# A two-layer transformer kernel on one core: twelve norm transposes go from TensorE to SyncE's DMA queue, and softmax pairs are allowed from an earlier point

## The chip, the cores and the metric

The kernel runs on one core of one Trainium2 chip. The metric is the device time of one execution in microseconds (us); a program's time is given as the median of its runs, and one execution of it is recorded by the hardware profiler. The engines are called PE (TensorE), DVE (VectorE), ACT (ScalarE), POOL (GpSimd) and SP (SyncE). SP only issues DMAs here.

## The reference, cut to what matters

```python
def attention(x):                      # A: wqkv, wo
    q, k, v = split(x @ wqkv)          # 32 heads of 16
    p = softmax(q @ k.T * 16 ** -0.5)
    return concat_heads(p @ v) @ wo

def dense(x):                          # B: w1, w2
    return relu(x @ w1) @ w2

x = A_x                                # [1, 2048, 512] bf16
for _ in range(2):
    x = x + attention(layernorm(x))
    x = x + dense(layernorm(x))
```

The inner width of `dense` is 1792. All inputs and the output are bf16. The softmax has 32 heads of 2048 x 2048 scores in each of the two layers: some 268 million exponentials in all, which is what most of the program's time goes to.

## The kernel before, in words

**Tiles.** The 2048 rows are cut into four chunks of 512 rows (`QS`), each of four row blocks of 128. In the second layer the last two chunks are cut in halves of 256 rows. Everything lives in SBUF: x as 16 tiles `x_t`, the transposed norm of a chunk as `xnT[j]` (128 x 4 x 512), keys as `ktp`, values as `vaug` (one tile of 128 rows for each key block, with columns of ones that give the softmax sums), and the attention output as `ot`.

**Norm.** Statistics of a row block come from DVE (`ln_stats`, L479), POOL works out the reciprocal root (`ln_seed`, L488 to L496), and DVE writes the normalised block into one of four buffers `xn0` to `xn3` (`ln_apply`, L526). In before, PE then transposes it, four 128 x 128 pieces a row block, into the PSUM bank `ps_f` (`ln_transpose`, L535), and DVE copies two row blocks at a time into `xnT[j]` (`ln_groups`, L583). As soon as PE has read an `xn` buffer, the next chunk's `ln_apply` may write it. The tag `("ln1", 0, j)` names the first norm of the first layer for chunk j; the code counts layers from 0. Chunk 0 of this norm is done by a short opening sequence of its own (L1146 to L1190), the other three go through `ln_rows` and, in before, `ln_groups`.

**Keys, values, queries.** `k_group`, `v_group` and `q_group` are groups of matmuls (L445) that read `xnT[j]`, write the one bank `ps_f`, and have it copied by DVE (L607 for keys, L643 for values, L657 for queries, which are masked and scaled on the way).

**Softmax by slots.** The main loop (from L1246) runs over slots. In each slot PE makes the scores of three blocks of 128 keys x 512 queries in one of two groups of three PSUM banks, `ps_s` (L1375), and ACT takes their exponentials with one instruction (L1384) into one of five buffers `e`. PE multiplies the result with the values (L963) into the bank `ps_o`. When a head is complete, DVE copies `ps_o` to `u` (L856, L875, L877), and a chain of small DMAs on SP's queue (`c<-u` at L882, `u<-c` at L905) and a broadcast DMA on POOL's queue (`r<-u` at L907) brings the reciprocal of the sums to all rows; DVE multiplies (L893).

**Pairs.** A slot may leave one of its three blocks to DVE. Then ACT's instruction covers 1024 columns instead of 1536. Two such blocks, from two slots two apart, form a pair: DVE computes an approximate exponential by steps named by their outputs: `lin` twice (L1070), `step` (L1111), `cube` (L1122), for some pairs a scaling (L1123), `step` again (L1111), and `cube` again (L1126). PE then adds three products to `ps_o` for each block of a pair, with `lin`, `step` and `cube`, in place of one with `e`. A condition in the main loop (L1273) decides whether a slot may begin a pair. In before, in the first layer, pairs are free only when the values of all 16 row blocks are made (`("v", 0, 15) in made`); until then a pair may begin only when no other is in work and the first keys of chunk 1 are there.

**Who sets the order.** Each engine runs its instructions in the order in which the program issues them. A planner in the kernel's Python code writes that order: it keeps its own clocks for PE and DVE (`now_pe`, `now_dve`), adds fixed costs for each task, and notes in `made` when each key will be there. `task` puts work into DVE's list, `mark` notes a key with a lag, `at` asks for the time of keys, `fill_pe` starts waiting groups on PE where their keys are made in time. These clocks only decide the order of the instructions; the chip's semaphores decide when they run.

**SP's queue at the start.** SP issues the loads of x (L176), of `wqkv`, `wo` and `w2` (L194, 1792 KB), and the first four blocks of `w1` (L695), in that order. The next DMA that SP issues in before is the first `c<-u`.

Of the kernel before, what the change touches and what calls it, by code (L numbers as in the profile page):

```python
# [25 lines left out]
def kernel(  # L26
# [10 lines left out]
    nc = tc.nc  # L37
    P = 128
# [13 lines left out]
    NQS = S // QS  # L52
    TPC = QS // P
# [17 lines left out]
    NP = 5  # L71
# [7 lines left out]
    FLOOR = 0.56  # L79
    C_LAG, R_LAG, U_LAG = 3600.0, 10500.0, 3000.0  # L80
    VLAG = 1
    RSTD_LAG = 4000.0
    AHEAD = (8.0, 8.0)
    LATE = 0.0
# [3 lines left out]
    PAIR_PACE = 2  # L88
# [47 lines left out]
    xnT = [sb([P, NDC, QS], BF16, f"xnT{j}") for j in range(NQS)]  # L136
# [104 lines left out]
    now_dve = [0.0]  # L241
# [3 lines left out]
    made = {}  # L245

    def mark(key, engine="dve", lag=0.0):
        made[key] = (engine, (now_pe if engine == "pe" else now_dve)[0] + lag)
# [38 lines left out]
    def task(cost, fn, makes=(), deps=(), place=None):  # L287
        t = {"cost": cost, "fn": fn, "makes": makes, "deps": deps}
        dve_q.insert(len(dve_q) if place is None else place, t)
        maker.update({k: t for k in makes})  # L290
# [178 lines left out]


    ln_seq = []

    def ln_n(tag):
        return ln_seq.index(tag) % 2
# [49 lines left out]
    def ln_apply(tag, tt, i):  # L524
        n = ln_n(tag)
        nc.vector.tensor_scalar(  # L526
            out=xnbuf[i][:], in0=x_t[tt][:],
            scalar1=mv[n][:, i, 0:1], scalar2=ya_[n][:, i : i + 1],
            op0=ALU.subtract, op1=ALU.mult,
        )  # L530

    def ln_transpose(tag, i, b=None, at_bank=None):
# [7 lines left out]
        mark(("xT", tag, i), "pe")  # L540
        return pt[:, 0 : NDC * P].rearrange("p (c f) -> p c f", c=NDC)

    def ln_rows(tag, tt, n, i):

        if tag not in ln_seq:
            ln_seq.append(tag)
        at_tag = ln_seq.index(tag)
        prev = ln_seq[at_tag - 1]
        rows_of_prev = chunks[prev[1:]][1]
        before_that = ln_seq[at_tag - 2] if at_tag > 1 else None  # L550
        old = each(chunks[before_that[1:]][1], "xn", before_that) if at_tag > 1 else []
        if ("st", tag, i) not in made:
            task(720, lambda: ln_stats(tag, tt + i, i), [("st", tag, i)], old)
        if i == n - 1:

            def rstd():
                ln_seed(tag, n)
                mark(("rs", tag, 3), lag=RSTD_LAG)

            task(0, rstd, [("rs", tag, 3)], each(n, "st", tag) + old)  # L560
            for k in range(n):
                task(
                    325, lambda k=k: ln_apply(tag, tt + k, k), [("xn", tag, k)],
                    [("xT", prev, k)] * (k < rows_of_prev) + [("rs", tag, 3)],
                )

# [33 lines left out]
    def each(n, *key):  # L600
        return [key + (i,) for i in range(n)]
# [174 lines left out]
    def rest_of_chunk(l, j):  # L776

        if (l, j) == (1, LAST - 2):
            for ft in range(NF):
                home = (  # L780
                    w1buf[((l * NQS + LAST) * NF + ft) % NW1] if ft < NW1
                    else (kt01 + kt2)[(ft - NW1) // 2][:, ft % 2, :].rearrange(
                        "p (c f) -> p c f", c=NDC
                    )
                )
                w1_last.append(home)
                if ft >= NW1:
                    w1_to_load.append((home, ft))
        b = before(l, j)
        xj, a, w = columns(l, j)  # L790
        n = w // P
        war_h = each(chunks[b][1], "z", *b) if b else []
        work[0:0] = [o_group(l, j, i) for i in range(n)] + ln_groups(
            ("ln2", l, j), xnT[xj], a, n, []
        )
        gs = [h_group(l, j, ft, war_h) for ft in range(0, NF, QS // w)]
        gs += [z_group(l, j, i) for i in range((l, j) == (1, LAST - 1), n)]
        if l == 0:
            gs += ln_groups(("ln1", 1, j), xnT[j], 0, TPC, [])
            gs.append(k_group(1, 0, j))  # L800
            gs += [v_group(1, kb) for kb in range(j * TPC, (j + 1) * TPC)]
            gs += [k_group(1, T, j) for T in range(1, 4)]
        return gs
# [388 lines left out]
    for j in range(1, NQS):  # L1192
        tag = ("ln1", 0, j)
        for i in range(TPC):
            ln_rows(tag, j * TPC, TPC, i)
        work.extend(k_group(0, T, 0) for T in FIRST_K[j])
        work.extend(ln_groups(tag, xnT[j], 0, TPC, []))
        work.append(k_group(0, 0, j))
        work.extend(v_group(0, kb) for kb in range(j * TPC, (j + 1) * TPC))
        if j == 1:  # L1200
            work.extend(k_group(0, T, 1) for T in range(1, MID))
# [44 lines left out]
    while units:  # L1246
# [22 lines left out]
        if len(banked) == W and pair_at in (None, no):  # L1269
            mine = banked[-1][0][0]  # L1270
            if pair_at == no:
                half, take = 1, pairs[-1]["sg"]
            elif (not pairs or pair_no[0] + 1 - pairs[0]["n"] < NP) and ((mine['l'] or ("v", 0, 15) in made or not pairs and ("k", 0, 0, 1) in made) and (not mine['l'] or ('k', 1, 0, NQS - 1) in made or pace < PAIR_PACE)):  # L1273
                queued = sum(t["cost"] for t in dve_q if "chain" in t)
                waiting = sum(t["cost"] for t in dve_q if at(t["deps"], "dve") is not None)
                others = sum(
                    t["cost"] for t in dve_q
                    if "chain" not in t and at(t["deps"], "dve") is not None
                )
                ends = max(now_dve[0] + others, now_pe[0] + 2600.0) + SPREAD * (queued + CHAIN)  # L1280
                if now_dve[0] + waiting < now_pe[0] + BACKLOG:
                    here = segs.index(mine)
                    first = max(here, segs.index(pairs[-1]["sg"])) if pairs else here
                    ahead = [x[0][0] for x in itertools.islice(units, 64 + 2 * 64)]
                    for n, sg in enumerate(segs[first : here + FAR]):
                        till = sum(x is sg or segs.index(x) < segs.index(sg) for x in ahead)
                        if (
                            sg["l"] == mine["l"] and ahead.count(sg) + (sg is mine) > 1
                            and at([("q", sg["n"])], "pe") is not None
                            and ends < now_pe[0] + till * QS * 0.84 - 1300.0  # L1290
                        ):
                            half, take = 0, sg
                            break
            if half is not None:
                other = [pairs[-1]["blocks"][0][0][2]] if half else []
                of_take = [x for x in banked if x[0][0] is take]
                third = half == 0 or all(y[1] in THIRD for y in pairs[-1]["blocks"][0])
                fit = next(
                    (
                        x for x in of_take[::-1]  # L1300
                        if third and x[0][2] not in other
                        and all(("third", y[0]["l"], y[1]) in made for y in x)
                    ), None
                )
                far = None
                if third and not fit:
                    far = next(
                        (
                            x for x in units if x[0][0] is take
                            and x[0][2] not in heads(banked[:-1]) + other  # L1310
                            and all(
                                ("third", y[0]["l"], y[1]) in made
                                and ("k", y[0]["l"], y[0]["T"], y[1] // TPC) in made for y in x
                            )
                        ), None
                    )
                if far:
                    units.remove(far)
                    units.appendleft(banked.pop())
                    x = far  # L1320
                elif fit or of_take:
                    x = fit or next((x for x in of_take[::-1] if x[0][2] not in other), of_take[-1])
                    banked.remove(x)
                else:
                    units.appendleft(banked.pop())
                    x = take_unit(heads(banked) + other, take)
                if True:
                    for sg, kb, g in x:
                        run_until(("k", sg["l"], sg["T"], kb // TPC))
                banked.append(x)  # L1330
                pair_at = no + 2 if half == 0 else None
# [206 lines left out]
```

The softmax here doesn't subtract the row's maximum and nothing guards it: scores larger than these inputs give would overflow.

## Time and profile before

| | us |
|---|---|
| median of 9 runs | 1593.5 |
| lowest and highest of the 9 | 1592.07, 1598.37 |
| the profiled execution, its own time | 1592.13 |
| its span in the profile | 1590.3 |
| busy in the span: ACT, DVE, PE, POOL | 1552.2, 1490.1, 1432.9, 100.0 |

The profile's page gives busy times of each engine, then the span in 40 slices of about 40 us with a digit of tenths for each engine, then the chain of work that ended last (followed back from the last instruction to what released each one), then groups of instructions. A row of a group reads: line, engine, operation, output <- inputs, shapes, count | busy us, mean ns of one | idle us of the engine just before them and what ended it. Records of instructions that follow each other on an engine overlap a little, so that a group's count times its mean is more than its busy time. A line number is that of the kernel before.

### The profile page before, as it was taken

To read this page: it belongs to the slowest core of one execution; us is meant where nothing else is said; L and a number is where in the kernel's file an instruction comes from. 1 tells how busy PE (TensorE), PEld (TensorE's weight loads), DVE (VectorE), ACT (ScalarE), POOL (GpSimd) and SP (SyncE) were. 2 spreads that over 40 slices of the span, in tenths; PEclk is the share of its full clock that TensorE was granted. 3 is DMA by queue.
4 is the path that set the end of the run, shared out by engine and by line. 5 is a ranking of instruction groups with operands and counts; after the bars stand their busy time and mean duration, and the time that the engine had idled before them with its cause. 6 is when DMAs were issued, how large, how long until landed. Compare 5 with 4: busy or idle time off the path is not lost.

```text
span 1590.3 us, 45152 instructions
## 1 busy us (share of the span) xinstructions
PE 1432.9 (90%) x19801; PEld 538.4 (34%) x19801; DVE 1490.1 (94%) x2876; ACT 1552.2 (98%) x1383; POOL 100.0 (6%) x240
## 2 busy tenths in 40 slices
PE   8888888999999999899889998888999999999898
PEld 3332222223232233223223232223334444544454
DVE  6669999999999999999899999999999999999995
ACT  6999999999999999999999999999999999999994
POOL 2000001001010010100000000001000001010100
PEclk9999999999999999999999999999999999999999
DMA  5001100210011100120001100000210211314020
GB/s 166 2 1 23 20 11 9 48 29 10 8 22 41 23 15 4 27 49 11 14 2 25 24 2 1 2 4 9 52 27 15 41 32 24 77 21 85 13 60 18
DMA packets 115829, 42.42 MB, mean 27 GB/s; under 512 B 104784, under 2 KB 112720, under 8 KB 115632
## 3 DMA queue, kind: packets, MB, share of 16 engines
q1 hardware_dynamic: 101696, 26.21, 7.2%
q0 software_dynamic: 12592, 12.02, 4.2%
q8 instruction: 154, 2.52, 0.7%
q10 hardware_dynamic: 1344, 1.31, 0.2%
q14 instruction: 43, 0.35, 0.1%
HBM read 24.38 MB, written 2.10 MB: 17 GB/s over the span
## 4 chain that ended last, share of the span: by engine, by line
ACT 80%; PE 9%; DVE 8%; issue 2%; DMA 0%; POOL 0%; ACTq 0%; DVEq 0%
ACT e L1384 80%; PE ps_s L1375 3%; PE ps_f L445 2%; DVE lin L1070 2%; PE ps_o L963 2%; DVE step L1111 1%; DVE cube L1126 1%; PE ps_s L1437 1%; DVE cube L1122 1%; DVE ht L717 1%; PE ps_o L1144 1%; DMA r<-u 0%; DVE q L657 0%; DVE ot L893 0%; DVE stats L479 0%
## 5 line engine op out<-in xcount | busy, mean ns | idle before, releaser
L1384 ACT ACTIVATE e<-ps_s 128x1024 bf16<-128x1024 f32 (+1 forms) x1366 | 1543.5, 1364 | 6.7 <-PE ps_s L1375 6.0
L1375 PE MATMUL ps_s<-q,ktp 32*128 32x512 bf16 (+1 forms) x6121 | 605.1, 340 | 116.7 <-ACT e L1384 104.8
L963 PE MATMUL ps_o<-e,vaug 128*32 128x512 bf16 (+1 forms) x4252 | 501.2, 345 | 11.3 <-DVE u L877 4.8
L1070 DVE TENSOR_SCALAR lin<-ps_s 128x512 int16<-128x512 f32 x686 | 466.8, 684 | 30.7 <-PE ps_s L1375 25.5
L1375 PEld LDWEIGHTS <-ktp 32*128 32x128 bf16 x6121 | 199.4, 91 | 566.0 <-issue 422.1
L963 PEld LDWEIGHTS <-vaug 128*32 128x32 bf16 x6040 | 170.8, 94 | 296.7 <-issue 278.0
L1111 DVE TENSOR_SCALAR step<-lin 128x1024 int16<-128x1024 int16 x686 | 268.8, 418 | 0.9
L1122 DVE TENSOR_TENSOR cube<-step 128x1024 f16<-128x1024 bf16 x343 | 232.2, 681 | 1.6 <-PE ps_o L963 0.8
L1126 DVE TENSOR_TENSOR cube<-cube,lin 128x1024 bf16<-128x1024 f16 x343 | 232.0, 678 | 0.0
L445 PE MATMUL ps_f<-xnT,w 128*32 128x512 bf16 (+1 forms) x2016 | 147.1, 346 | 4.9 <-DVE ht L717 2.5
L963 PE MATMUL ps_o<-step,vaug 128*32 128x512 bf16 (+1 forms) x868 | 151.0, 340 | 0.0
L445 PE MATMUL ps_f<-w,ht 128*32 128x512 bf16 x1624 | 148.5, 381 | 1.1 <-DVE x L749 0.3
L963 PE MATMUL ps_o<-cube,vthird 128*32 128x512 bf16 (+1 forms) x816 | 144.5, 338 | 0.0
L963 PE MATMUL ps_o<-lin,vaug 128*32 128x512 bf16 (+1 forms) x868 | 122.9, 341 | 4.6 <-DVE u L877 2.6
L907 POOL DMA_DIRECT2D r<-u x59 | 42.7, 724 | 1191.7 <-DVE lin L1070 282.1
L445 PE MATMUL ps_f<-xnT,wqkv 128*32 128x512 bf16 (+1 forms) x1312 | 106.9, 360 | 5.6 <-DVE q L657 1.0
L445 PE MATMUL ps_f<-wo,ot 128*32 128x512 bf16 x960 | 91.7, 381 | 1.0 <-DVE x L681 0.9
L717 DVE TENSOR_SCALAR ht<-ps_f 128x512 bf16<-128x512 f32 x105 | 71.9, 684 | 2.4 <-PE ps_f L445 1.3
L445 PEld LDWEIGHTS <-w 128*32 128x32 bf16 x2016 | 57.7, 96 | 33.1 <-issue 17.7
L657 DVE TENSOR_TENSOR q<-ps_f,masks 128x1024 bf16<-128x1024 f32 (+1 forms) x51 | 53.6, 1051 | 10.9 <-PE ps_f L445 7.5
L445 PEld LDWEIGHTS <-ht 128*32 128x32 bf16 x1624 | 46.7, 96 | 27.4 <-issue 13.3
L963 PEld LDWEIGHTS <-vthird 128*32 128x32 bf16 x816 | 42.5, 95 | 34.3 <-issue 29.7
(103 smaller groups left out, 629.2 us busy)
## 6 DMA issues: line engine op xcount, KB each, us to landing
w<-in_B_w_dram SPq DMA_DIRECT2D x130, 128.0 KB
r<-u POOLq DMA_DIRECT2D x32, 256.0 KB, 7.4
r<-u POOLq DMA_DIRECT2D x27, 128.0 KB, 4.8
out_dram<-x SPq DMA_DIRECT2D x16, 128.0 KB
x<-in_A_x_dram SPq DMA_DIRECT2D x14, 128.0 KB
w<-in_B_w_dram SPq DMA_DIRECT2D x1, 1792.0 KB
ktp<-in_B_w_dram SPq DMA_DIRECT2D x10, 128.0 KB
wqkv<-in_A_wqkv_dram ACTq DMA_DIRECT2D x2, 512.0 KB
```

The lines of the kernel that those rows point to most:

```text
L445: nc.tensor.matmul(out[cols], lhsT[:, cols], rhs, start=i % k == 0, stop=i % k == k - 1, tile_position=(0, 32 * g), skip_group_check=True,)
L657: return nc.vector.tensor_mul(out=qbuf[n % 2][:, :, 0:w], in0=b.rearrange("p (e q) -> p e q", e=1).to_broadcast((P, 2, w)), in1=qmask.rear ...
L717: nc.vector.tensor_scalar(out=out, in0=sums, scalar1=0.0, scalar2=None, op0=ALU.max)
L907: nc.gpsimd.dma_start(out=r[:, 0:width], in_=bass.AP(tensor=sums.tensor, offset=sums.offset, ap=[list(sums.ap[0]), [0, 32], [1, width]],),)
L963: nc.tensor.matmul(ps_o[32 * g : 32 * g + 32, 0 : sg["w"]], values[:, 4 * sg["T"] + g, 2 * e : 2 * e + 32], rhs, start=g not in sg["begun" ...
L1070: first = nc.vector.tensor_scalar(out=lin[which][:, half * QS : (half + 1) * QS], in0=src, scalar1=EXP_BIAS, scalar2=0.0, op0=ALU.add, op1 ...
L1111: nc.vector.tensor_scalar(out=stair, in0=line, scalar1=keep, scalar2=put, op0=ALU.bitwise_and, op1=ALU.bitwise_or,)
L1122: (609, lambda: nc.vector.tensor_mul(out=power, in0=mantissa, in1=mantissa)),
L1126: (609, lambda: nc.vector.tensor_mul(out=power.bitcast(BF16), in0=power, in1=line.bitcast(BF16))),
L1144: nc.tensor.matmul(ps_o[:], ebuf[0][:, 0:P], ebuf[0][:, 0:QS], start=True, stop=True)
L1375: nc.tensor.matmul(b[:, a : a + sg["w"]], kt[32 * g : 32 * g + 32, kc : kc + P], qbuf[sg["n"] % 2][32 * g : 32 * g + 32, sg["e"], 0 : sg[" ...
L1384: ex = nc.scalar.activation(out=eb[:, 0 : place[m]], in_=b[:, 0 : place[m]], func=ACTF.Exp, scale=1.0 / (LOG2E * UNIT),)
```

## The change

It has two parts.

First, for the chunks 1, 2 and 3 of the first layer's first norm (rows 512 to 2047), the normalised row block is transposed by a DMA that SP issues, straight from `xn` into `xnT[j]`. These twelve DMAs take the place of 48 matmuls of PE and six copies of DVE. The planner takes `X_ISSUE` (1400 ns) for each in SP's queue and `X_LAG` (7500 ns) more until the keys `xT` (buffer `xn` may be written again) and `xnT` (the transposed block is there) are made. What waits for PE's transpose before now waits for the DMA's landing. All other norm transposes stay as they were.

Second, in the first layer pairs are free from the time when the values of the first six row blocks are made (`("v", 0, 5) in made`).

```diff
+    X_ISSUE, X_LAG = 1400.0, 7500.0
...
+    sp_free = [0.0]
...
+    def by_dma(tag):
+        return tag[:2] == ("ln1", 0) and tag[2] > 0
+
     def ln_rows(tag, tt, n, i):
...
+            def apply(k):
+                ln_apply(tag, tt + k, k)
+                if not by_dma(tag):
+                    return
+                _, l, j = tag
+                nc.sync.dma_start_transpose(
+                    out=xnT[j][:, :, k * P : (k + 1) * P], in_=xnbuf[k][:]
+                )
+                sp_free[0] = max(sp_free[0], now_dve[0]) + X_ISSUE
+                lag = sp_free[0] + X_LAG - now_dve[0]
+                mark(("xT", tag, k), lag=lag)
+                mark(("xnT", tag, k), lag=lag)
+
             for k in range(n):
                 task(
-                    325, lambda k=k: ln_apply(tag, tt + k, k), [("xn", tag, k)],
+                    325, lambda k=k: apply(k),
+                    [("xn", tag, k)] + [("xT", tag, k), ("xnT", tag, k)] * by_dma(tag),
                     [("xT", prev, k)] * (k < rows_of_prev) + [("rs", tag, 3)],
                 )
...
         if l == 0:
-            gs += ln_groups(("ln1", 1, j), xnT[j], 0, TPC, [])
+            if not by_dma(("ln1", 1, j)):
+                gs += ln_groups(("ln1", 1, j), xnT[j], 0, TPC, [])
...
         work.extend(k_group(0, T, 0) for T in FIRST_K[j])
-        work.extend(ln_groups(tag, xnT[j], 0, TPC, []))
+        if not by_dma(tag):
+            work.extend(ln_groups(tag, xnT[j], 0, TPC, []))
...
-            elif (not pairs or pair_no[0] + 1 - pairs[0]["n"] < NP) and ((mine['l'] or ("v", 0, 15) in made or not pairs and ("k", 0, 0, 1) in made) and (not mine['l'] or ('k', 1, 0, NQS - 1) in made or pace < PAIR_PACE)):
+            elif (not pairs or pair_no[0] + 1 - pairs[0]["n"] < NP) and ((mine['l'] or ("v", 0, 15) in made or ("v", 0, 5) in made or not pairs and ("k", 0, 0, 1) in made) and (not mine['l'] or ('k', 1, 0, NQS - 1) in made or pace < PAIR_PACE)):
```

## The prediction, made before the changed kernel was run

> **What bounds the kernel now.** I read the page's busy shares, slices and chain first. The chain is the work that ended last, followed back.
>
> ```profile
> PE 1432.9 (90%) x19801; PEld 538.4 (34%) x19801; DVE 1490.1 (94%) x2876; ACT 1552.2 (98%) x1383; POOL 100.0 (6%) x240
> ...
> DVE  6669999999999999999899999999999999999995
> ACT  6999999999999999999999999999999999999994
> ...
> ACT 80%; PE 9%; DVE 8%; issue 2%; DMA 0%; POOL 0%; ACTq 0%; DVEq 0%
> ```
>
> ScalarE (ACT) is full from the second slice (40 us) on, and the chain is mostly ACT. DVE has room in one place only: 6 tenths in the first three slices, to about 120 us. The chain in order of time says when ACT takes over:
>
> ```profile
> 28.87 76.02 ACT e L1384 x60
> 104.89 0.16 issue
> 105.05 55.84 ACT e L1384 x49
> ```
>
> From 28.87 us on the exponentials follow each other without a break: 60 slots in 76.02 us. Only shorter or fewer exponentials shorten this. Next, the stretch that the change works in beside a later one, by windows (us busy of each engine, instructions in brackets):
>
> ```profile
> 30.00:125.00 95.00, 83.65 (x990) 28.84 (x988) 63.19 (x110) 95.00 (x78) 2.64 (x6) 1.00 0.01 2
> 200.00:400.00 200.00, 179.85 (x2127) 57.96 (x2126) 194.92 (x370) 200.00 (x182) 14.03 (x26) 1.00 0.11 22
> ```
>
> Columns: window, length, PE, PEld, DVE, ACT, POOL, clock, DMA share, GB/s. In 30 to 125 us ACT is full while DVE idles 95 - 63.19 = 31.8 us. In 200 to 400 us DVE is 97.5% busy and ACT still lacks nothing: a DVE that full has fed ACT before.
>
> **What the Trainium skill says.** "TensorE: Matmul & The Clock Gate", Part 4: PE-mode transpose: a TensorE transpose lands in PSUM and needs a DVE copy after. The trace agrees: 219 ns transposes at L535, then 679 ns copies at L583. "Advanced Engine Details and Errata", X-Bar Transpose (TRN2): transposing DMAs are as fast as regular ones. "DMA: Bandwidth & Descriptors", Latency and other measured facts: 261 GB/s for one transpose kernel. Same page, Issuing engines are not separate DMA queues: DMAs from every issuing engine share 16 engines. No transposing DMA is in the trace of before, so neither speed can be checked; the sharing shows in a DMA share of 0.96 from 13 to 24 us.
>
> **The change part by part.** I count from the order in which the two built programs' instructions stand.
>
> 1. *Pairs.* A pair takes two 512-column blocks from ACT to DVE. Before has 343, after 350: exponentials of 1536 columns fall from 679 to 665, those of 1024 rise from 686 to 700, still 1366 in all. By slot 83 after is 16 short slots ahead (31 against 15); from slot 100 on its lead stays exactly 14, and the later pattern of short slots is the same. Hence all the gain must appear before about 140 us. Rows by form:
>
> ```profile
> L1384 ACT ACTIVATE e<-ps_s 128x1536 bf16<-128x1536 f32 x679 | 1020.3, 1576 | 4.7 <-PE ps_s L1375 4.1 <-PE ps_o L963 0.3
> L1384 ACT ACTIVATE e<-ps_s 128x1024 bf16<-128x1024 f32 x686 | 740.3, 1155 | 2.0 <-PE ps_s L1375 2.0
> ```
>
> 1576 - 1155 = 421 ns a block, on the path: 14 x 0.421 = **5.9 us off**.
>
> 2. *DVE work added and taken.* By these rows:
>
> ```profile
> L1070 DVE TENSOR_SCALAR lin<-ps_s 128x512 int16<-128x512 f32 x686 | 466.8, 684 | 30.7 <-PE ps_s L1375 25.5
> L1111 DVE TENSOR_SCALAR step<-lin 128x1024 int16<-128x1024 int16 x686 | 268.8, 418 | 0.9
> L1122 DVE TENSOR_TENSOR cube<-step 128x1024 f16<-128x1024 bf16 x343 | 232.2, 681 | 1.6 <-PE ps_o L963 0.8
> L1126 DVE TENSOR_TENSOR cube<-cube,lin 128x1024 bf16<-128x1024 f16 x343 | 232.0, 678 | 0.0
> ...
> L583 DVE COPY xnT<-ps_f 128x1024 bf16<-128x1024 bf16 x29 | 19.7, 679 | 2.2 <-PE ps_f L535 2.1
> ...
> L1123 DVE TENSOR_SCALAR cube<-cube 128x1024 f16<-128x1024 f16 x25 | 10.3, 416 | 0.2
> ```
>
> 14 x 0.684 + 14 x 0.418 + 7 x 0.681 + 7 x 0.678 + 3 x 0.416 = 26.2 us added; 6 copies at L583, 4.1 us, gone. Net +22.1 us into a stretch that idles 31.8 us and gets 5.9 shorter: 85.3 of 89.1 us, 96%. The cover is that idle time; records overlap, so 22.1 is rather too much. By the later windows it fits: 0 on the path. Were it gone, each DVE us too many would be an ACT us.
>
> 3. *PE.* 48 transposes go (4.2 us by their row in 30 to 130 us); 28 more value matmuls come (14 fewer on e, 14 more on each of lin, step and cube). 226 such rows were busy 30.6 us there, so 28 x 0.135 = 3.8 us. A wash; PE at 94% of the shortened stretch beside 92% at 300 to 400 us, where ACT idled 0. Taken as 0.
>
> 4. *The transposes.* Twelve DMAs of 128 KB join SP's queue, after the last w1 load and ahead of the first c of a normalisation (114.89 us before). That queue is empty between, and the DMA share from 26 us is 0.01, so nothing waits behind them but each other. What they delay is decided by the first four:
>
> ```profile
> 22.66 1.37 DVE L526 TENSOR_SCALAR xn<-x,mv,ya 128x512 bf16<-128x512 bf16 x4
> ...
> 14.52 8.97 SPq L695 DMA_DIRECT2D w<-in_B_w_dram  x4
> ...
> 37.08 0.39 PE L1375 MATMUL ps_s<-q,ktp 32*128 32x512 bf16 x3
> ```
>
> xn of rows 512 to 1023 is ready at 24.03, SP is free at 23.49, and the w2 and w1 data ahead are through at about 25 us (DMA share 0.66, then 0.08). In the new order PE stands, after the scores of slot 17 (37.1 us by the last line), before a K group that needs all four. PE can wait there to about 38 us, since exponential 18 starts at 39.5 us. **Budget: 38 - 24 = 14 us.** From below, by the skill's 261 GB/s, 128 KB take 0.5 us; with everything ahead drained at 25 us they are down by 27 us. From above, the nearest row is a POOL DMA of 128 KB, 4.8 us from issue to landing; strictly one after another, 4 x 4.8 = 19.2 us, 5 us over. I take issues that overlap, and use the 1.4 us an issue and 7.5 us to landing that the new planner code assumes, which no run shows, as a cautious case: 23.5 + 5.6 + 7.5 = 36.6 us. Inside: **0**, with 0 to 5 us for the range.
>
> The same landings free xn: the next four applies (L526) wait for them in place of PE's transposes, at about 33 us (after the copy to ht that ends at 32.7 us in before). Behind them on DVE stand the K copies of head groups 2 and 3, and behind those PE's scores of head group 2, from about 43 us on: some 8 us to spare. Blocks 2 and 3 have slack by their positions: their first uses follow slots 37 (63 us) and 58 (90 us), their xn are made by about 37 and 47 us.
>
> 5. *Later.* Same ACT order, somewhat other DVE and PE interleaving. ACT's waits after 200 us are about 4 us in all; I allow +0.5, between -4 and +3.
>
> Sum: -5.9 + 0 + 0 + 0 + 0.5 = -5.4. The profiled execution took 1592.1 us (1590.3 its span, 1.8 around it): 1586.7. It lies 1.4 below the median of 1593.5, so the median goes to about **1588**.
>
> **The rivals.**
> (a) *DVE or PE becomes the bound in the new dense stretch.* 96% leaves 3.8 us, and the stretch also copies K and V from the single bank ps_f, so PE and DVE wait for each other as they do now. Against: 125 to 150 us has the same mix, DVE 24.94 of 25, ACT 25.00. Price: 2 to 4 us of the gain back, 1590 to 1592.
> (b) *Slower: the transposes are late.* If each takes the 7.4 us that the 256 KB POOL DMA takes to land, and they do not overlap, the fourth lands at 24 + 29.6 = 53.6 us, 15.6 over: net +9.7 us, about 1603; blocks 2 and 3 would add to it. It turns from gain to loss at (14 + 5.9) / 4 = 5 us a transpose. For it: DMA transposes are unseen here. Against: SP's plain loads, 128 KB and larger, moved at 291 GB/s from 13 to 24 us.
> (c) *No effect*: the later stages lose what the early one gains. Against: one continuous ACT chain passes an early gain on. 1593.
>
> **How the numbers follow.** Forecast 0.65, (a) 0.17, (b) 0.11, (c) 0.07. A measurement here tells about 0.2%, 3.2 us, from no change. All of the forecast and a third of (a) are faster by more, the rest of (a) and (c) within, (b) slower: 0.71, 0.18, 0.11. Range: from all the gain plus 4 us of later waits, 1583.5, to past (a) and (c) and half-late transposes, 1596.
>
> **What would show it.** Right: ACT without a gap from about 29 us; 665 and 700 exponentials; DVE at 9 tenths from the second slice; first lin near 41 us in place of 47.4; slot 100 about 6 us earlier; transposes landing before 37 us. Wrong: PE waiting for a DMA at the K groups; DVE waiting for a DMA at L526 (by its old number); ACT idle by microseconds before 140 us; or a gain at 140 us that is gone at 1560.

## The result and the profile after

The changed kernel takes 1588.01 us (median of 10 runs, 1585.71 to 1590.45); before, over all runs now taken, 1593.67 us. The ratio is 0.9964, 95% interval 0.9955 to 0.9972: 5.7 us faster, forecast 5.5. The profiled execution took 1585.71 us, its span is 1583.9 us. Line numbers below are those of the kernel that the fence is of; the changed kernel's lie up to 21 higher than those of before, those of some other kernels a few more.

The page of the changed kernel, busy shares, slices and chain:

```profile
PE 1428.1 (90%) x19781; PEld 535.9 (34%) x19781; DVE 1507.2 (95%) x2915; ACT 1546.2 (98%) x1383; POOL 100.4 (6%) x240
...
DVE  7899999999999999999899999999999999999994
ACT  7999999999999999999999999999999999999993
...
ACT 79%; DVE 9%; PE 8%; issue 2%; DMA 1%; POOL 0%; ACTq 0%; DVEq 0%
```

The hole in DVE's slices, 6 6 6 before, is 7 8 9 now. ACT is still what the chain consists of, and has 6.0 us less to do.

The two windows of the prediction again (window, length, then busy us of PE, PEld, DVE, ACT, POOL, with instructions in brackets; clock, DMA share, GB/s):

```profile
30.00:125.00 95.00, 85.72 (x1033) 27.63 (x1026) 85.88 (x158) 94.82 (x83) 2.46 (x5) 1.00 0.08 16
200.00:400.00 200.00, 180.12 (x2140) 57.86 (x2133) 195.76 (x371) 200.00 (x182) 13.80 (x26) 1.00 0.11 22
```

In 30 to 125 us DVE went from 63.19 to 85.88 us busy and ACT lost 0.18 us of 95. The same 95 us now hold 83 exponentials where there were 78.

Groups by form, ACT and DVE:

```profile
L1405 ACT ACTIVATE e<-ps_s 128x1536 bf16<-128x1536 f32 x665 | 1003.2, 1573 | 4.5 <-PE ps_s L1396 3.8 <-PE ps_o L983 0.3
L1405 ACT ACTIVATE e<-ps_s 128x1024 bf16<-128x1024 f32 x700 | 754.5, 1153 | 0.0
...
L1090 DVE TENSOR_SCALAR lin<-ps_s 128x512 int16<-128x512 f32 x700 | 476.3, 684 | 25.5 <-PE ps_s L1396 19.5
...
L602 DVE COPY xnT<-ps_f 128x1024 bf16<-128x1024 bf16 x23 | 15.6, 680 | 0.1
```

The counts are as worked out: 665 and 700 exponentials, 14 more `lin`, 6 copies fewer, and a block still costs 1573 - 1153 = 420 ns.

The transposes, by the timeline of SP, DVE and PE (start us, us):

```profile
23.24 26.35 SPq L571 DMA_TRANSPOSE xnT<-xn  x12
...
32.35 0.73 DVE L528 TENSOR_SCALAR xn<-x,mv,ya 128x512 bf16<-128x512 bf16 x2
...
36.95 0.69 DVE L626 CAST ktp<-ps_f 128x512 bf16<-128x512 f32 x1 [1.16 <-PE ps_f L446]
37.63 0.69 DVE L876 COPY ht<-ps_o 128x512 f32<-128x512 f32 x1
...
37.70 1.05 PE L446 MATMUL ps_f<-xnT,wqkv 128*32 128x512 bf16 x16
```

The first four are issued from 23.24 us on, 1.2 us each after a first one of 1.76, and their data are through at 30.0 us (the DMA share of the half microsecond after is 0). The rewriting of `xn` at 32.35 us and the K group at 37.70 us wait for no DMA.

Where the time went can be counted slot by slot. I take the start of the 161st exponential, at 206.33 us before; up to there everything in the changed kernel's exponentials that differs by plan has happened, and in the others all but one block at most. It comes 5.63 us earlier after. The one ahead of it begins these two lines, before and after, 5.63 us apart as well:

```profile
205.00 2.50 ACT L1384 ACTIVATE e<-ps_s 128x1536 bf16<-128x1536 f32 x2
199.37 2.50 ACT L1405 ACTIVATE e<-ps_s 128x1536 bf16<-128x1536 f32 x2
```

The expected lead of the 161st is the number of blocks moved off ACT so far times 0.42 us. What is missing from that is, to within 2 us, ACT's stops up to there, beyond the 0.4 us that ACT stops before (5.4 us of stops where pairs_only misses 5.7, 20.7 where v3_pairs_only misses 22.6). The same sum for every kernel:

| kernel | blocks moved by then | their worth, us | start of exponential 161 against before, us | missing, us | ratio of the whole to before |
|---|---|---|---|---|---|
| changed kernel | 14 | -5.9 | -5.6 | 0.3 | 0.9964 (0.9955 to 0.9972) |
| the same again (after_again) | 14 | -5.9 | -5.5 | 0.4 | 0.9967 (0.9958 to 0.9976) |
| dma_only | 9 | -3.8 | -4.1 | -0.3 | 0.9982 (0.9970 to 0.9995) |
| pairs_only | 15 | -6.3 | -0.6 | 5.7 | 1.0011 (0.9998 to 1.0024) |
| v4 | 18 | -7.6 | -3.8 | 3.8 | 0.9997 (0.9983 to 1.0011) |
| v3 | 23 | -9.7 | -0.3 | 9.4 | 1.0019 (1.0008 to 1.0030) |
| v3_pairs_only | 21 | -8.8 | +13.8 | 22.6 | 1.0085 (1.0068 to 1.0103) |
| dve_extra | 14 | -5.9 | -2.7 | 3.2 | 0.9991 (0.9979 to 1.0003) |
| delay1 | 14 | -5.9 | -5.3 | 0.6 | 0.9970 (0.9961 to 0.9978) |
| delay3 | 14 | -5.9 | +5.8 | 11.7 | 1.0049 (1.0033 to 1.0065) |
| lag | 18 | -7.6 | -0.2 | 7.4 | 1.0013 (0.9997 to 1.0030) |
| pool_third | 19 | -8.0 | -3.8 | 4.2 | 0.9983 (0.9974 to 0.9992) |

### The profile page after: what moved, and what is told of

It is laid out like the page before. It is cut to its first block, busy times and chain, and to the rows that moved or that the text cites. A ratio compares the mean times of both kernels' runs of the same rounds, so it can differ in the third digit from the quotient of the medians.

```text
span 1583.9 us, 45187 instructions
## 1 busy us (share of the span) xinstructions
PE 1428.1 (90%) x19781; PEld 535.9 (34%) x19781; DVE 1507.2 (95%) x2915; ACT 1546.2 (98%) x1383; POOL 100.4 (6%) x240
## 4 chain that ended last, share of the span: by engine, by line
ACT 79%; DVE 9%; PE 8%; issue 2%; DMA 1%; POOL 0%; ACTq 0%; DVEq 0%
ACT e L1405 79%; PE ps_s L1396 3%; DVE lin L1090 2%; PE ps_f L446 2%; PE ps_o L983 2%; DVE step L1131 1%; PE ps_s L1458 1%; DVE cube L1146 1%; DVE cube L1142 1%; DVE ht L736 1%; DMA r<-u 0%; DVE q L676 0%; DVE stats L481 0%; DVE ot L913 0%; DVE u L897 0%
## 5 line engine op out<-in xcount | busy, mean ns | idle before, releaser
L1090 DVE TENSOR_SCALAR lin<-ps_s 128x512 int16<-128x512 f32 x700 | 476.3, 684 | 25.5 <-PE ps_s L1396 19.5
L1131 DVE TENSOR_SCALAR step<-lin 128x1024 int16<-128x1024 int16 x700 | 273.8, 418 | 0.8
L1142 DVE TENSOR_TENSOR cube<-step 128x1024 f16<-128x1024 bf16 x350 | 237.0, 681 | 1.6 <-PE ps_o L983 0.8
L1146 DVE TENSOR_TENSOR cube<-cube,lin 128x1024 bf16<-128x1024 f16 x350 | 236.8, 678 | 0.0
```

What stands on the lines that cost most here:

```text
L1090: first = nc.vector.tensor_scalar(out=lin[which][:, half * QS : (half + 1) * QS], in0=src, scalar1=EXP_BIAS, scalar2=0.0, op0=ALU.add, op1 ...
L1131: nc.vector.tensor_scalar(out=stair, in0=line, scalar1=keep, scalar2=put, op0=ALU.bitwise_and, op1=ALU.bitwise_or,)
L1142: (609, lambda: nc.vector.tensor_mul(out=power, in0=mantissa, in1=mantissa)),
L1146: (609, lambda: nc.vector.tensor_mul(out=power.bitcast(BF16), in0=power, in1=line.bitcast(BF16))),
```

## The experiments

The prediction says that the moved blocks are the gain, and that DVE has room for them. Theory A takes that literally: only the blocks count. Theory B says that the room has to be made, and that taking the transposes off PE and DVE makes it.

**Each half alone.** pairs_only keeps the earlier point and puts the transposes back on TensorE:

```diff
     def by_dma(tag):
-        return tag[:2] == ("ln1", 0) and tag[2] > 0
+        return False
```

> The changed kernel with the twelve transposes back on TensorE; the earlier point for pairs (values of row blocks 0 to 5 made) is kept. The planner then still makes 700 short exponentials, 14 blocks moved off ScalarE, as in the changed kernel. Theory A (only the moved blocks count, 0.42 us each): -5.9 us, about 1587.8. Theory B (taking the transposes and their copies off PE and DVE is what keeps ScalarE fed in the dense stretch): DVE has 4 us more work there than in the changed kernel, ScalarE waits for scores before 140 us, 2 to 4 us of the gain are lost: 1590 to 1592.

dma_only keeps the transposes and puts back the old point (the part of the condition that differs):

```diff
-((mine['l'] or ("v", 0, 15) in made or ("v", 0, 5) in made or not pairs and
+((mine['l'] or ("v", 0, 15) in made or not pairs and
```

> The changed kernel with the old point for pairs (all 16 value blocks made); the twelve DMA transposes are kept. Because keys come earlier, the planner makes 694 short exponentials, 8 blocks more than before. Theory A: 8 x 0.42 = -3.4 us, about 1590.3. Theory B (the relief of PE and DVE is the larger part of the gain): -5 us or more, 1588.5 or below. If DMA transposes do nothing for the time and cost something: 1593 or above.

pairs_only moves as many blocks as the changed kernel and gains nothing: 1.0011. Theory A falls there, and Theory B was too mild: not 2 to 4 us of the gain are lost but all of it. dma_only moves 8 in all and gains 0.18%, about 2.9 us, near the 3.4 of its blocks and short of Theory B's 5. So taking the transposes off PE and DVE gives nothing that can be seen beyond the blocks that it lets the planner move; the blocks set what is to be had, and in pairs_only ACT gives it back. The halves do not add up: by the ratios about +1.7 and -2.9 us, together -5.7. The windows of 30 to 125 us of dma_only and of pairs_only, ACT's waits in pairs_only (us in total, times, longest us), and the stretch around 98 us from its chain in order of time (start us, us, what):

```profile
30.00:125.00 95.00, 84.93 (x1029) 28.61 (x1019) 71.89 (x126) 95.00 (x80) 2.58 (x5) 1.00 0.07 13
```

```profile
30.00:125.00 95.00, 83.26 (x996) 28.48 (x984) 79.52 (x145) 89.56 (x76) 1.41 (x4) 1.00 0.01 2
```

```profile
ACT e L1405 <- PE ps_o L983: 3.2, 2, 2.0
ACT e L1405 <- PE ps_s L1396: 2.2, 2, 1.9
```

```profile
97.61 0.60 DVE lin L1090
98.21 0.59 DVE ht L874
98.80 0.60 DVE cube L1142
99.40 0.61 DVE xnT L602
100.02 0.04 issue
100.06 1.07 PE ps_f L446 x16
101.15 0.70 DVE ktp L626
101.86 0.05 issue
101.90 0.39 PE ps_s L1396 x3
102.29 0.55 PE ps_o L983 x8
```

In pairs_only ACT is busy 89.56 us of 95, though DVE with 79.52 us is less busy than in the changed kernel. The chain shows why an engine that is not full can still be the bound. The copy to `xnT` stands in DVE's queue behind the steps of a pair. PE needs that copy to free the bank `ps_f` before its next group, DVE has to copy the keys out of the same bank, and the scores of the next slot, which stand behind that group in PE's order, start only after that copy of the keys, at 101.90 us. Such a round trip waits for DVE's queue twice. With the transposes done by DMA, six of these round trips and the copies in them do not exist. ACT stops for 1.88 us after this one. Its two other long stops, 1.21 and 1.99 us at 113 to 117 us, come after the last copy to `xnT`: there PE and DVE wait for each other around copies of values and keys from the same bank, and the chain holds no exponential from 79.57 to 116.66 us.

**How much of it is DVE's time.** dve_extra gives the changed kernel six idle multiplications as long as the six copies, without any use of `ps_f`:

```diff
+    extra = rbuf[2][:].bitcast(BF16)
+    nc.gpsimd.memset(rbuf[2][:], 0.0)
...
             mark(("v", l, kb))
+            if l == 0 and kb in (4, 6, 8, 10, 12, 14):
+                nc.vector.tensor_mul(out=extra, in0=extra, in1=extra)
```

> The changed kernel, same order, with six more multiplications of 128x1024 bf16 on DVE (about 0.68 us each, after the copies of value blocks 4, 6, 8, 10, 12 and 14), as much DVE time as the six copies that the change removed, but no transposes on PE and no use of the bank ps_f. If DVE time is what the transposes by DMA save: ScalarE stops for 3 to 6 us before 120 us, 1591 to 1594. If it is the round trips PE, ps_f, DVE, PE that they save: at most 1.5 us lost, 1588 to 1590.

```profile
30.00:125.00 95.00, 83.65 (x994) 26.71 (x993) 86.25 (x159) 92.75 (x80) 2.57 (x6) 1.00 0.07 14
```

ACT falls to 92.75 us of 95. The 4.1 us more of DVE time put exponential 161 back by 2.9 us (-5.6 to -2.7), and the ratio is 0.9991: the stretch has no room for the six copies. That lies between the two forecasts, nearer to 3 to 6 us than to at most 1.5. pairs_only misses 5.7 us, this one 3.2, the changed kernel 0.3: of the 5.4 us that the transposes on PE cost, about 2.9 come with as much DVE time alone. The other 2.5 are consistent with the round trips, but the multiplications do not stand where the copies stood and the two kernels' orders also differ, so that share is argued and not measured by itself.

**More pairs still.** The same condition one and two row blocks earlier, and the latter also without the DMA transposes (again only the part that differs):

```diff
-or ("v", 0, 5) in made
+or ("v", 0, 4) in made      # v4; 3 in v3 and v3_pairs_only
```

> The changed kernel with pairs free one row block earlier (values of row blocks 0 to 4 made): 704 short exponentials, 18 blocks more than before, 4 more than the changed kernel, hardly any of them in the first 20 slots. Blocks alone: -7.6 us against before, 1586. If the stretch is already full at 14 blocks, ScalarE's stops eat it: 1588 to 1591.

> The changed kernel with pairs free two row blocks earlier, once the values of row blocks 0 to 3 are made; the DMA transposes stay. 710 short exponentials, 24 blocks more than before, 7 of them in the first 20 slots. Theory A: 24 x 0.42 = -10.1 us, about 1583.6. Rival: between 25 and 45 us DVE also has statistics, K and V copies to do, and pairs there make PE and ScalarE wait: ScalarE gaps of some us before 60 us, and 1586 to 1588 at best, no better than the changed kernel.

> Pairs free from the values of row blocks 0 to 3, all transposes on TensorE. 706 short exponentials, 20 blocks more than before. Theory A: 20 x 0.42 = -8.4 us, about 1585.2. Theory B: the densest early stretch with the six copies on DVE; ScalarE waits, 1587 to 1590.

All three move more blocks and none beats the changed kernel; each is also slower than the forecast that allowed for ACT's stops. v4 loses 3.8 of its 7.6 us by exponential 161. v3 moves 23 blocks by then and is slower than before; its window shows DVE hardly busier than the changed kernel's 85.88 us, and ACT at 86.85:

```profile
30.00:125.00 95.00, 82.67 (x1000) 26.54 (x992) 87.06 (x164) 86.85 (x77) 2.60 (x9) 1.00 0.06 13
```

The longest wait that its list of waits from 25 to 60 us holds for ACT's exponentials is in a like ping-pong of PE and DVE, here around the bank `ps_o` and the steps of a pair in place of `ps_f`:

```profile
ACT e L1405 <- PE ps_o L983: 4.4, 3, 3.6
...
PE ps_o L983 <- DVE ht L876: 1.7, 4, 0.8
...
PE ps_o L983 <- DVE cube L1146: 1.4, 1, 1.4
```

With the transposes by DMA, 86 to 87 us of 95 is what DVE reaches in this stretch, with 14 blocks or with 23. And without the transposes by DMA the early point of v3 costs 22.6 us, against 9.4 with them.

**How late the transposes may be.** delay1 and delay3 put one and three more transposing DMAs, into tiles not yet in use, ahead of each of the first four. All engines but SP keep their order:

```diff
...
+                for d in range(3 if j == 1 else 0):      # 1 in delay1
+                    nc.sync.dma_start_transpose(
+                        out=spare[3 * k + d].rearrange("p (c f) -> p c f", c=NDC), in_=xnbuf[k][:]
+                    )
                 nc.sync.dma_start_transpose(
                     out=xnT[j][:, :, k * P : (k + 1) * P], in_=xnbuf[k][:]
```

> The changed kernel with one more transposing DMA, into a tile that is not yet used, ahead of each of the first four. The order of all engines stays. In the changed kernel these four are issued from 23.2 us, 1.2 us each, and their data are through at about 29.7 us; with eight the fourth should land at about 35 us. Budget theory (PE needs it at about 38 us): no loss against the changed kernel, ratio to before 0.996 to 0.998. Rival (the landings already lie on the path through the writes to xn or the K groups): 4 to 5 us lost.

> The same with three more ahead of each of the first four: sixteen DMAs, the last landing at about 45 us, 7 us past the budget. Budget theory: PE waits for a DMA at the first K group of chunk 1, ScalarE stops there for about 6 to 8 us, and the kernel is some 6 to 8 us slower than the changed one, at about 1594 to 1596. Rival (other work hides it): within 2 us of the changed kernel.

delay1 costs nothing (0.9970). delay3 is slower than before, and loses 11 to 12 us against the changed kernel, not 6 to 8. Its timeline of DVE, PE and PEld (PE's weight loads), the last of the four transposing DMAs from its chain, and two windows tell the route:

```profile
35.52 0.41 DVE L528 TENSOR_SCALAR xn<-x,mv,ya 128x512 bf16<-128x512 bf16 x1 [2.84 <-DMA xnT<-xn]
35.85 0.68 DVE L631 CAST ktp<-ps_f 128x512 bf16<-128x512 f32 x1
...
36.58 0.83 PE L446 MATMUL ps_f<-xnT,wqkv 128*32 128x512 bf16 x12 [1.61 <-DVE ktp L631]
...
40.80 0.41 DVE L528 TENSOR_SCALAR xn<-x,mv,ya 128x512 bf16<-128x512 bf16 x1 [4.27 <-DMA xnT<-xn]
46.01 0.41 DVE L528 TENSOR_SCALAR xn<-x,mv,ya 128x512 bf16<-128x512 bf16 x1 [4.79 <-DMA xnT<-xn]
46.34 0.68 DVE L631 CAST ktp<-ps_f 128x512 bf16<-128x512 f32 x1
...
47.08 1.90 PE L446 MATMUL ps_f<-xnT,wqkv 128*32 128x512 bf16 x16 [8.14 <-DVE ktp L631]
```

```profile
45.97 0.10 PEld L446 LDWEIGHTS <-wqkv 128*32 128x32 bf16 x1 [7.34 <-DMA xnT<-xn]
```

```profile
43.44 2.49 DMA xnT<-xn
```

```profile
40.00:47.00 7.00, 0.00 (x0) 0.10 (x1) 1.40 (x4) 0.58 (x1) 0.00 (x0) 0.70 0.48 96
47.00:52.00 5.00, 4.92 (x40) 1.24 (x39) 2.17 (x5) 2.38 (x2) 0.00 (x0) 0.50 0.40 82
```

Two waits run side by side, and both end with the same DMA. The first weight load of the K group waits 7.34 us for the transposed rows, until 45.97 us: the wait that the budget theory named. DVE waits for the buffer `xn`, which the DMA has not finished reading; behind that write in DVE's queue stands a key copy from `ps_f`, and the K group needs that bank, free at 47.02 us. So DVE's route ends last, by 1.1 us. ACT stands still for 9.0 us ahead of the scores of slot 18. DVE's route had already stopped ACT for 1.05 us at slot 16: the key copy at 35.85 us, behind the `xn` write of 35.52 us, held up a group that needs no row of chunk 1. The rest of the excess is PE's speed. In the 5 us after PE's idle time the granted clock is 0.50, and the 16 matmuls of the group take 1.90 us in place of the changed kernel's 1.05; slot 20 stops ACT for another 0.92 us. An estimate from these figures for the 11.4 us that exponential 161 is later than in the changed kernel: about 7 for PE's wait for rows, as forecast, 2 for DVE's route and 2 for the low clock.

**Can the planner do better.** lag sets the planner's constants to what the trace shows (1.3 us an issue, 1.5 us more to landing); pool_third puts the scalings of value tiles by a third on POOL:

```diff
-    X_ISSUE, X_LAG = 1400.0, 7500.0
+    X_ISSUE, X_LAG = 1300.0, 1500.0      # lag
...
-            225, lambda: nc.vector.tensor_scalar(
+            0, lambda: nc.gpsimd.tensor_scalar(      # pool_third
```

> The changed kernel with the planner's constants set to what its trace shows for these DMAs: 1.3 us an issue and 1.5 us more until the data are there (in place of 1.4 and 7.5). 704 short exponentials, 4 blocks more than the changed kernel. Blocks alone: 1.7 us better than the changed kernel. If the stretch has no DVE time left for them: equal to it within 2 us, with ScalarE stops before 120 us.

> The changed kernel with the eight scalings of value tiles by a third (0.3 us each on DVE, four of them in the dense stretch) on POOL. 704 short exponentials, 4 blocks more, DVE relieved by 1.2 us there. Blocks plus relief: 1.5 to 2.5 us better than the changed kernel. If POOL's scaling is slow, PE waits for it and ScalarE stops: 0 to 3 us worse.

> The changed kernel itself, once more, beside the two others: ratio to before 0.996 to 0.997. Its profile tells whether the 2 us that the first profile gained after 400 us belong to the kernel (then they are there again) or to that execution (then they are not).

Neither beats the changed kernel. In lag the chain has the first transpose on it:

```profile
23.33 3.61 DMA xnT<-xn
```

It lands 3.6 us after its issue, with the loads of `w2` and `w1` ahead of it in the queue; the planner counted on 2.8 and put the next write of `xn` right there, at 27.07 us (32.35 us in the changed kernel), ahead of copies that PE needs. ACT stops 1.4 us at slot 10, where the changed kernel stops 0.3. The 8.9 us that the changed kernel's planner counts, over three times the 2.5 us of delay3, had kept that write out of the way. Most of what lag loses comes later: 4.9 us of stops from 61 to 120 us, with four more blocks in the full stretch. pool_third misses 4.2 us of its 8.0 by exponential 161. A scaling took POOL 1.6 to 2.1 us, DVE 0.3, but no engine waited for one from 30 to 125 us; that the full stretch has no use for the four blocks more is the likely cause, and is not shown.

after_again repeats the result, 0.9967, and its early lead: -5.5 us at exponential 161. The further 2 us that the first profile gained after 400 us are not there.

## Why the prediction was right, step by step

**Pairs: right.** 14 blocks at 420 ns. The lead is 5.6 us from slot 100 on, 5.4 of it gathered after the first ten slots.

**DVE: the mechanism right, the sum too large.** The prediction added 22.1 us to 63.19 and called it rather too much. Up to 119 us, the window shortened by the gain, DVE was busy 79.9 us: 16.7 more. It concluded from 96% against 97.5% in a later window that the stretch had room. It had, but only just, and a share of busy time was a poor measure of how much: dve_extra adds 4.1 us to a stretch with some 9 us of idle DVE and loses 2.9 us. That the cover was enough is thus in part luck. The idle time left is mostly spent waiting for PE, and is not free for other work.

**What the transposes are for: undervalued.** In the prediction's sum they were 4.1 us less on DVE and a wash on PE, beside pairs that carry the gain. pairs_only shows that the pairs alone carry nothing. What happens there is rival (a): DVE and PE become the bound and wait for each other around `ps_f`. The change escapes that rival because it takes six copies and six trips through that bank away; of the 5.4 us between the two kernels about 2.9 go with the copies' time (dve_extra), and the rest is put down to the trips without being measured. The prediction named (a) and gave 2 to 4 us as its price; in the kernel where it happens it is 5.7. The range and the number held because the change brings both halves; the prediction did not see that the first needs the second.

**Transposes in time: right; the budget: wrong in one step.** The fourth was put between 27 us and 36.6, used cautiously; its data were through at 30.0 us. No run here tests that DMAs of several queues share the engines: from 13 to 24 us before, SP's queue alone moved 3.18 of the 3.21 MB. The step that failed is the one that gave the writes to `xn` "some 8 us to spare", with the K copies behind them needed only by scores from 43 us on. What needs those copies first is the bank: they free `ps_f` for the group at 37.7 us. So the limit was about 36.5 us, not 38 (in delay1 the fourth lands at 34.0 + 2.5 = 36.5 us and DVE waits 0.8 us without harm). In the changed kernel 6 us of slack remained and the error cost nothing. In delay3 it cost about 2 us; the other 2 of the expectation's miss, 6 to 8 us against 11 to 12, go with the clock that fell in PE's idle time, which the budget did not have.

**PE: near enough.** 94% was foreseen for the shortened stretch, 90% measured (80.3 of 89 us).

**Later: about nothing in the median, more in one profile than was allowed.** +0.5 was taken, -4 to +3 allowed. The medians differ by 5.7 us and exponential 161 by 5.6. After exponential 161 the first profile gains 2.4 us by the last exponential and then loses 1.6 in the tail, where ACT waits 6.2 us for PE before its first copy of x, 4.6 before. The second profile of the same program loses 6.9 us after exponential 161, so that its last exponential starts 1.4 us later than before: by itself the sign of being wrong that the prediction named last. The 17 runs that go with it still give 0.9967, so that is scatter between executions, not the change. Of the signs of being right, ACT had one gap, of 0.15 us at 63.53 us, and DVE's "9 tenths from the second slice" failed: the first slices read 7 8 9. The others came true.

## What to carry to other kernels

Where one engine bounds, moving work off it pays only if the helper can take it without being late for a third engine: count the round trips through a shared buffer, not only busy shares. A change in two halves should be tried by halves; here the half that looked like the gain gives nothing without the half that looked like tidying, and the tidying alone gives about half. And when a wait is added, follow everything behind it in that engine's queue to the first resource that somebody else needs, a bank as well as a value.

## What the runs showed of the hardware

A transposing DMA of 128 x 512 bf16 from SBUF to SBUF held SP's queue for 1.2 to 1.3 us and landed 2.5 us after its issue (delay3), 3.6 with large loads ahead (lag); a plain DMA issue of a `c<-u` held it 0.55 us before. Issued one after another the transposes are bound by the issue: in delay3 the queue issues them back to back while the DMA share is 0.48 (40 to 47 us), 131 KB each 1.3 us, some 100 GB/s. That is not the 261 GB/s of the Trainium skill's page "DMA: Bandwidth & Descriptors" (Latency and other measured facts), which the prediction's estimate from below used. Nor were they as fast as regular DMAs, as the Trainium skill has it ("Advanced Engine Details and Errata", X-Bar Transpose (TRN2)): plain loads from DRAM, of 128 KB and larger, ran at 291 GB/s from 13 to 24 us before. Larger transposes were not tried.

In delay3 PE made no matmul from 38.9 to 47.1 us. The granted clock averages 0.70 from 40 to 47 us, 0.50 from 47 to 52 and 1.00 from 58 us on: this stop of PE cost more than its own length.

The scatter between executions of one program goes with the granted clock of TensorE. The two profiles of the changed kernel, by cores and spans:

```profile
core 0: 1583.9 us, clock 0.997
```

```profile
core 0: 1591.9 us, clock 0.989
```

In the first ten runs too, those at 0.997 took 1585.71 to 1586.6 us and those at 0.993 took 1588.88 and 1590.45. In the profile at 0.989 ACT waits 11.1 us for scores, in the one at 0.997 3.8 us, nearly all of the difference after 200 us. So a change of 2 us can't be read from one profile here; the first 200 us, which repeat to 0.2 us, can.
